# First FFT stage of the later batches with the data stationary, turned by DMA transposes instead of through DRAM

## The chip, the cores and the metric

The kernel runs on one core of a Trainium2 chip. The metric is the device time of one execution in microseconds. Three executions of the kernel before took 783.91, 784.35 and 784.50 us, median 784.35.

The engines that the text names: PE (TensorE, matrix multiplications; "PEld" are its weight loads), DVE (VectorE), ACT (ScalarE), POOL (GpSimd), and SP (SyncE), which only issues DMA transfers here. A matmul has a stationary operand, which is loaded into the array beforehand, and a moving operand, which streams through it; the result lands in PSUM, and DVE or ACT must carry it ("evacuate" it) into SBUF, the working memory.

## The reference

Eight sequences of 3008 tokens with 256 channels are filtered in the frequency domain along the sequence; the result goes through a two-layer network with a gated activation.

```
X = rfft(x, axis=1)                       # x: 8 x 3008 x 256
y = irfft(X * (filt_r + 1j*filt_i), n=3008, axis=1)
h = y.reshape(24064, 256) @ w_in          # 256 -> 2048
g = h / (1 + exp(-beta * h))
out = g @ w_out                           # 2048 -> 256, float32
```

## The kernel before

**The network** is the bulk. The 24064 tokens are cut into 47 blocks of 512, the 2048 hidden units into 16 slices of 128. One step is one slice of one block: two matmuls of 512 columns into hps (L842), a SILU on ACT into gT (L857), and, two steps later (LAG), four matmuls of 256 columns that add gT times a slice of w_out onto acc (L897). After 16 steps acc is evacuated into ost and stored. The matmul order on PE is the order in which the Python loop emits it; nothing is reordered by a scheduler.

**The filtering** of one batch feeds the blocks of that batch and is woven into the steps of the batch before it. The transform of 3008 points is factored as 94 rows of 32 (S = 47 x 64, J = 32 columns j):

1. s1 (L623): for each j, the 94 rows are multiplied with the 94x96 table t1, which gives 96 = 4 x 24 rows (four parts a for 24 frequencies k).
2. s23 (L644): for each frequency k, the 128 = 32 x 4 rows (j, a) are multiplied with a 128x128 table (L651), then with the filter (p_t, q_t on DVE, v_t on POOL), then with the table of the inverse (L677).
3. s4 (L692): the last stage back to the sequence (last4, L553, matmul L556).

Between 1 and 2 the data must change its partition axis: s1 leaves the 96 rows (a, k) on the partitions, s23 wants (j, a) there. The kernel before does this through DRAM. Two columns j at a time go through one matmul with the table stationary and 512 columns moving (L629); the evacuation puts them into an a1 tile of eight columns j, and SP writes it to the DRAM scratch d1 (L634). Once all four are written, a2_read (L636) reads d1 back in four groups of six frequencies with (j, a) on the partitions (L641). Between 2 and 3 there is a like round trip through d2 (L682, L689), which stays as it is.

Batch 0 is different: it works alone at the start, and its first stage (first1, L298) already holds the data stationary (L305) and turns it with PE transposes (turn_a, L396). It isn't changed.

**The order.** A plan written by hand says in which step each piece goes (place, L706; the calls from L764 on). For batch 1: s1 in steps 3 to 14, then in the next step a2_read(1) and, right behind it on SP, the last eight of the twelve loads of the real filter (uf, L741; each 256 KB, frequencies in groups of eight); s23 starts in step 20. For batch 2: s1 in steps 52 to 66, a2_read in step 75. For the later ones, with a the first step of the batch before: s1 from a + 48, a2_read at a + 68, and s23 from 3 steps after the next batch's own start, a span of about 30 steps. SP's queue runs in order: d1 and d2 transfers, filter loads and the stores of ost share it.

**Buffers that the steps touch.** apool has three a1 tiles, a2pool five a2 tiles (four for a batch), ostp three ost tiles (a block fills two), fpsum three PSUM banks for all filter stages, opsum three for acc.

**The end.** The last block has four accumulators of 256 columns (h = 0 to 3); ACT evacuates 0 and 3, DVE 1 and 2; the third store is issued from ACT's queue, the others from SP.

Of the kernel before, what the change touches and what calls it, by code (L numbers as in the profile page):

```python
# [9 lines left out]
P = 128  # L10
# [3 lines left out]
F32 = mybir.dt.float32  # L14
BF16 = mybir.dt.bfloat16
# [13 lines left out]
NK = 24  # L29
J = 32  # L30
KG = 6
NG = NK // KG
JG = 8
# [6 lines left out]
def kernel(  # L40
# [10 lines left out]
    nc = tc.nc  # L51

    B, S, D = x.shape
# [5 lines left out]
    NDC = D // P  # L59
    NFB = FF // P  # L60
    NP = 2 * N1
    KP = 4 * NK
# [6 lines left out]
    dpool = ctx.enter_context(tc.tile_pool(name="dram_scratch", bufs=2, space=bass.MemoryType.DRAM))  # L69

    def pool(name, bufs, **kw):
        return ctx.enter_context(tc.tile_pool(name=name, bufs=bufs, **kw))
# [1 line left out]
    consts = pool("consts", 1)  # L74
    wpool = pool("wpool", 1)
    xpool = pool("xpool", 1)
    apool = pool("apool", 3)
    ypool = pool("ypool", 2)
    a2pool = pool("a2pool", 5)
    pqpool = pool("pqpool", 3)  # L80
# [5 lines left out]
    fpsum = pool("fpsum", 3, space=bass.MemoryType.PSUM)  # L86
# [4 lines left out]
    t1 = consts.tile([NP, KP], BF16, name="t1", tag="t1")  # L91
    t4 = consts.tile([KP, NP], BF16, name="t4", tag="t4")
    t1b = consts.tile([NP, KP], BF16, name="t1b", tag="t1b")
# [13 lines left out]
    def evac(dst, src, on_act, scale=None):  # L107
        if on_act:
            nc.scalar.activation(dst, src, ACT.Copy, scale=1.0 if scale is None else scale)  # L109
        elif scale is None:  # L110
            nc.vector.tensor_copy(dst, src)  # L111
        else:
            nc.vector.tensor_scalar_mul(dst, src, scale)  # L113
# [132 lines left out]
    half = fixed("half", -0.5)  # L246
# [289 lines left out]
    ys = {}  # L536
    ys[0] = ypool.tile([P, NDC, NK * P], BF16, name="y", tag="y")
    zz0 = {}
    zz0[0] = apool.tile([KP, JG, D], BF16, name="zz", tag="a1")


    def turn_z(g, i, on_act=False):
# [67 lines left out]
    st = {}  # L610

    def start(b):
        d1 = dpool.tile([J, KP, D], BF16, name="d1", tag="d1")
        d2 = dpool.tile([J, KP, D], BF16, name="d2", tag="d2")
        st[b] = {
            "x": xs.pop(b),
            "d1r": d1.rearrange("j r d -> r j d"),
            "d2r": d2.rearrange("j r d -> r j d"),
            "d1c": d1.rearrange("j (a k) d -> (j a) k d", a=4),
            "d2c": d2.rearrange("j (a k) d -> (j a) k d", a=4),  # L620
        }

    def s1(b, i, on_act):  # L623
        s = st[b]
        g, jj = divmod(2 * i, JG)
        if jj == 0:
            s["a1"] = apool.tile([KP, JG, D], BF16, name="a1", tag="a1")
        ps = fpsum.tile([P, 512], F32, name="ps1", tag="f")
        nc.tensor.matmul(  # L629
            ps[:KP], lhsT=t1[:], rhs=s["x"][:, 2 * i : 2 * i + 2, :], start=True, stop=True  # L630
        )
        evac(s["a1"][:, jj : jj + 2, :], ps[:KP], on_act)
        if jj + 2 == JG:
            nc.sync.dma_start(s["d1r"][:, g * JG : (g + 1) * JG, :], s["a1"][:])  # L634

    def a2_read(b):  # L636
        s = st[b]
        s["a2"] = []
        for h in range(NG):
            t = a2pool.tile([P, KG, D], BF16, name="a2", tag="a2")  # L640
            nc.sync.dma_start(t[:], s["d1c"][:, h * KG : (h + 1) * KG, :])  # L641
            s["a2"].append(t)

    def s23(b, i):  # L644
        s = st[b]
        if i < NK // 2:
            k0 = 2 * i
            g, kk = divmod(k0, KG)
            ps = fpsum.tile([P, 2, D], F32, name="ps2", tag="f")
            for e in range(2):  # L650
                nc.tensor.matmul(  # L651
                    ps[:, e, :],
                    lhsT=t2[:, k0 + e, 3:5, :].rearrange("p c k -> p (c k)"),
                    rhs=s["a2"][g][:, kk + e, :],
                    start=True,
                    stop=True,
                )
            p_t = pqpool.tile([P, 2, D], F32, name="p_t", tag="p_t")
            q_t = pqpool.tile([P, 2, D], F32, name="q_t", tag="q_t")
            v_t = vpool.tile([P, 2, D], BF16, name="v_t", tag="v_t")  # L660
            ks_ = slice(k0, k0 + 2)
            nc.vector.tensor_tensor(p_t[:], ps[:], frr[:, ks_, :], ALU.mult)  # L662
            nc.vector.scalar_tensor_tensor(  # L663
                q_t[M:P], ps[:M], -1.0, fri[M:P, ks_, :], ALU.mult, ALU.mult
            )
            nc.vector.tensor_tensor(q_t[:M], ps[M:P], fri[M:P, ks_, :], ALU.mult)  # L666
            nc.gpsimd.tensor_tensor(v_t[:], p_t[:], q_t[:], ALU.add)  # L667
            s["v", i] = v_t
        if i >= VLAG:
            k0 = 2 * (i - VLAG)  # L670
            g, kk = divmod(k0, KG)
            if kk == 0:
                s["z"] = zpool.tile([P, KG, D], BF16, name="z", tag="z")
            v_t = s.pop(("v", i - VLAG))
            ps = fpsum.tile([P, 2, D], F32, name="ps3", tag="f")
            for e in range(2):
                nc.tensor.matmul(  # L677
                    ps[:, e, :], lhsT=t3[:, k0 + e, :], rhs=v_t[:, e, :], start=True, stop=True
                )
            evac(s["z"][:, kk : kk + 2, :], ps[:], True)  # L680
            if kk + 2 == KG:
                nc.sync.dma_start(s["d2c"][:, g * KG : (g + 1) * KG, :], s["z"][:])  # L682
# [114 lines left out]
            place(a + 68, a + 68, [lambda b=b: a2_read(b + 1)], per=9)  # L797
        place(a + 63, a + 78, u4(b))

    def store(t0, tn, ost, eng=nc.sync):  # L800
        if t0 >= S:
            eng.dma_start(
                out[t0 : t0 + tn, :].rearrange("(c p) d -> p c d", p=P), ost[:, : tn // P, :]
            )
            return
        for tb in range(tn // P):
            c0 = t0 + tb * P
            c1 = c0 + P
            while c0 < c1:
                lo = (c0 - t0) % P  # L810
                if c0 >= S:
                    nc.sync.dma_start(out[c0:c1, :], ost[lo : lo + c1 - c0, tb, :])
                    break
                g, r = divmod(c0, CLS)
                n = min(c1 - c0, CLS - r)
                nc.sync.dma_start(
                    AP(
                        out.tensor,
                        out.offset + (r // JC * J + g * JC) * D,
                        [[J * D, n // JC], [D, JC], [1, D]],  # L820
                    ),
                    ost[lo : lo + n, tb, :],
                )
                c0 += n
# [4 lines left out]
    for s in range(len(steps) + LAG):  # L829
# [34 lines left out]
        if s >= LAG:  # L864
# [40 lines left out]
            if fb == NFB - 1:  # L905
                for h, a in enumerate(acc):
                    if h * per % 2 == 0:
                        ost = ostp.tile([P, 2, D], F32, name="ost", tag="ost")
                    c = h * per % 2
                    on_act = h == 0 and i < 6 or last and h in (0, 3)  # L910
                    evac(ost[:, c : c + per, :], a[:], on_act)
                    eng = nc.scalar if last and h == 2 else nc.sync
                    store(t0 + h * per * P, per * P, ost[:, c : c + per, :], eng)


# [28 lines left out]
```

## Time and profile before

| | us |
|---|---|
| median of 3 executions | 784.35 |
| the profiled execution | 783.44 |
| its span, first to last instruction | 781.4 |
| PE busy | 772.4 |
| ACT busy | 595.8 |
| DVE busy | 390.8 |
| L857 SILU on ACT | 515.6 |
| L897 and L842 matmuls | 451.4 and 447.7 |
| L629 matmuls, 112 of them | 42.0 |
| a1 evacuations on DVE, 96 of them | 65.9 |

Busy matmul time is the union of intervals that overlap, since each matmul is counted until its result has drained; what a matmul takes from PE is the distance to the start of the next. The granted TensorE clock was full in the whole run. Transfers issued by SP show their issue in the trace, not their landing; a landing is seen only where an engine waits for it.

### The profile page before, as it was taken

The page shows a single profiled execution, that of the slowest core. Times are in us where ns is not written, and L with a number is a line of the kernel's source. Part 1 is how long each engine was busy: PE and PEld are TensorE (multiplying, and loading weights), DVE is VectorE, ACT ScalarE, POOL GpSimd, SP SyncE. Part 2 cuts the span into 40 slices and gives each one's busy share as a digit, 9 for nine tenths or more (in the row PEclk, how much of TensorE's full clock was granted, in tenths as well). Part 3 has the DMA queues.
Part 4 walks back from the last instruction along what each step waited for, and adds up shares of the span by engine and source line. Part 5 has one row for each costly group of instructions (what it writes and reads, how often), then busy time and mean ns, then how long its engine had stood idle before and what let it go on. Part 6 is the DMA issues. An engine that isn't in the chain of part 4 may idle for free.

```text
span 781.4 us, 15550 instructions
## 1 busy us (share of the span) xinstructions
PE 772.4 (99%) x6108; PEld 548.5 (70%) x6108; DVE 390.8 (50%) x640; ACT 595.8 (76%) x926; POOL 142.9 (18%) x145
## 2 busy tenths in 40 slices
PE   8999999999999999999999999999999999999997
PEld 5866667766777667876678766787667776776665
DVE  7847646746446553474635746277453751401001
ACT  7887887886678867787677876778767787677776
POOL 7523401420013100231002310034000330000000
PEclk9999999999999999999999999999999999999999
DMA  8968673517801286022951238412471114100101
GB/s 190 261 168 226 161 219 123 132 63 202 222 28 68 79 206 188 29 91 92 198 159 37 86 124 181 140 56 88 118 199 55 48 68 128 55 29 28 55 28 54
DMA packets 84473, 91.45 MB, mean 117 GB/s; under 512 B 4562, under 2 KB 74596, under 8 KB 83442
## 3 DMA queue, kind: packets, MB, share of 16 engines
q1 hardware_dynamic: 81536, 74.61, 31.0%
q0 software_dynamic: 2720, 15.73, 10.4%
q8 instruction: 47, 0.77, 0.4%
q14 instruction: 26, 0.21, 0.1%
q10 hardware_dynamic: 144, 0.13, 0.0%
HBM read 57.16 MB, written 46.66 MB: 133 GB/s over the span
## 4 chain that ended last, share of the span: by engine, by line
PE 95%; ACT 2%; DVE 1%; DMA 1%; issue 0%; DVEq 0%; ACTq 0%; POOL 0%; POOLq 0%; SPq 0%
PE acc L897 41%; PE hps L842 41%; PE ps L629 3%; PE ps L556 3%; PE ps L677 2%; PE ps L651 2%; PE psz L477 1%; ACT a L109 0%; DMA a<-d 0%; DMA d<-a 0%; ACT gT L857 0%; PE pb L403 0%; ACT a_t L109 0%; ACT t L280 0%; ACT r L284 0%
## 5 line engine op out<-in xcount | busy, mean ns | idle before, releaser
L857 ACT ACTIVATE gT<-hps,beta_sb 128x512 bf16<-128x512 f32 x752 | 515.6, 687 | 172.4 <-PE hps L842 160.7
L897 PE MATMUL acc<-wout_sb,gT 128*128 128x256 bf16 x3008 | 451.4, 272 | 0.0
L842 PE MATMUL hps<-y,win_sb 128*128 128x512 bf16 (+8 forms) x1730 | 447.7, 351 | 0.0
L897 PEld LDWEIGHTS <-gT 128*128 128x128 bf16 x3008 | 285.6, 98 | 128.8 <-issue 0.3
L842 PEld LDWEIGHTS <-win_sb 128*128 128x128 bf16 x1730 | 164.9, 98 | 24.4 <-issue 0.2
L667 POOL TENSOR_TENSOR v_t<-p_t,q_t 128x512 bf16<-128x512 f32 x84 | 106.6, 1269 | 389.8 <-DVE q_t L666 382.7
L111 DVE COPY ost<-acc 128x512 f32<-128x512 f32 (+1 forms) x88 | 56.2, 677 | 191.4 <-PE acc L897 188.2
L111 DVE CAST a<-ps 96x512 bf16<-96x512 f32 x96 | 65.9, 687 | 85.2 <-PE ps L629 84.6
L113 DVE TENSOR_SCALAR y<-ps 128x376 bf16<-128x376 f32 (+1 forms) x115 | 61.6, 543 | 58.8 <-PE ps L556 58.8
L662 DVE TENSOR_TENSOR p_t<-ps,frr 128x512 f32<-128x512 f32 x84 | 58.1, 691 | 36.9 <-PE ps L651 31.6
L666 DVE TENSOR_TENSOR q_t<-ps,fri 64x512 f32<-64x512 f32 x84 | 58.3, 694 | 1.2
L663 DVE SCALAR_TENSOR_TENSOR q_t<-ps,fri 64x512 f32<-64x512 f32 x84 | 57.5, 684 | 1.1
L556 PEld LDWEIGHTS <-zz 96*128 96x128 bf16 x512 | 35.3, 97 | 29.1 <-issue 0.3
L109 ACT ACTIVATE z<-ps 128x512 bf16<-128x512 f32 x84 | 49.5, 589 | 0.0
L629 PE MATMUL ps<-xg,t 94*96 94x512 bf16 x112 | 42.0, 381 | 0.1
L556 PE MATMUL ps<-t,zz 96*128 96x94 bf16 x448 | 36.7, 204 | 0.0
L677 PE MATMUL ps<-v_t,t 128*128 128x256 bf16 x168 | 32.1, 273 | 0.4 <-ACT y L109 0.4
L651 PE MATMUL ps<-a,t 128*128 128x256 bf16 x168 | 32.1, 273 | 0.3 <-DMA a<-d 0.3
L120 POOL DMA_DIRECT2D xg<-in_x_dram x22 | 12.1, 552 | 100.9 <-PE acc L897 96.8
L651 PEld LDWEIGHTS <-t 128*128 128x128 bf16 x168 | 15.6, 98 | 14.7 <-DMA a<-d 0.8
L629 PEld LDWEIGHTS <-t 94*96 94x96 bf16 x112 | 13.7, 123 | 12.0
L677 PEld LDWEIGHTS <-t 128*128 128x128 bf16 x168 | 16.2, 98 | 6.9 <-ACT y L109 0.7
(118 smaller groups left out, 194.9 us busy)
## 6 DMA issues: line engine op xcount, KB each, us to landing
out_dram<-ost SPq DMA_DIRECT2D x80, 256.0 KB
d<-a SPq DMA_DIRECT2D x28, 384.0 KB
a<-d SPq DMA_DIRECT2D x28, 384.0 KB
d<-z SPq DMA_DIRECT2D x28, 384.0 KB
zz<-d SPq DMA_DIRECT2D x28, 384.0 KB
xg<-in_x_dram POOLq DMA_DIRECT2D x6, 1280.0 KB, 10.4
frr<-in_filt_r_dram SPq DMA_DIRECT2D x12, 256.0 KB
out_dram<-ost SPq DMA_DIRECT2D x19, 128.0 KB
```

The source lines that it names most:

```text
L111: nc.vector.tensor_copy(dst, src)
L113: nc.vector.tensor_scalar_mul(dst, src, scale)
L556: nc.tensor.matmul(ps[:, e, :NP], lhsT=zz[:, jj + e, dc * P : (dc + 1) * P], rhs=tab[:], start=True, stop=True,)
L629: nc.tensor.matmul(ps[:KP], lhsT=t1[:], rhs=s["x"][:, 2 * i : 2 * i + 2, :], start=True, stop=True)
L651: nc.tensor.matmul(ps[:, e, :], lhsT=t2[:, k0 + e, 3:5, :].rearrange("p c k -> p (c k)"), rhs=s["a2"][g][:, kk + e, :], start=True, stop=True,
L662: nc.vector.tensor_tensor(p_t[:], ps[:], frr[:, ks_, :], ALU.mult)
L666: nc.vector.tensor_tensor(q_t[:M], ps[M:P], fri[M:P, ks_, :], ALU.mult)
L667: nc.gpsimd.tensor_tensor(v_t[:], p_t[:], q_t[:], ALU.add)
L677: nc.tensor.matmul(ps[:, e, :], lhsT=t3[:, k0 + e, :], rhs=v_t[:, e, :], start=True, stop=True)
L842: nc.tensor.matmul(hps[:, pos - t0 : pos - t0 + ln], lhsT=win_sb[:, dc, fb * P : (fb + 1) * P], rhs=ys[b][:, dc, n0 : n0 + ln], start=(dc ...
L857: nc.scalar.activation(gT[:, :tn], hps[:, :tn], ACT.Silu, scale=beta_sb[:, fb : fb + 1])
L897: nc.tensor.matmul(acc[tb // per][:, tb % per, :], lhsT=g_[:, tb * P : (tb + 1) * P], rhs=wout_sb[:, f_, :], start=(f_ == 0 and tb % per = ...
```

## The change

First stage, batches 1 to 7: for each group of four columns j and each half of the channels (dc), four matmuls hold 128 channels of x stationary (94x128) and move the 94x96 table t1b, whose columns are ordered (k, a). The result has the channels on the partitions. One evacuation of 128x384 puts it into an a1 tile of its half, ordered (k, j, a). For batch 1 the two halves alternate; for later batches the first half is done whole, then the second. In a2_read eight DMA transposes, issued by SP, turn each half's six blocks of 128x128 per frequency group into a2, where (j, a) is on the partitions; L651 reads the two halves of a2 as one operand of 256 columns. d1 is gone. apool has two tiles, each now holding half the channels of a whole batch.

At the end, accumulator 3 is evacuated in two halves, one on DVE and one on ACT, and the third store goes out from SP like the others.

```diff
-    apool = pool("apool", 3)
+    apool = pool("apool", 2)
...
     def start(b):
-        d1 = dpool.tile([J, KP, D], BF16, name="d1", tag="d1")
...
-            "d1r": d1.rearrange("j r d -> r j d"),
+            "a1": [apool.tile([P, NK * P], BF16, name="a1", tag="a1") for _ in range(NDC)],
...
     def s1(b, i, on_act):
         s = st[b]
-        g, jj = divmod(2 * i, JG)
-        if jj == 0:
-            s["a1"] = apool.tile([KP, JG, D], BF16, name="a1", tag="a1")
-        ps = fpsum.tile([P, 512], F32, name="ps1", tag="f")
-        nc.tensor.matmul(
-            ps[:KP], lhsT=t1[:], rhs=s["x"][:, 2 * i : 2 * i + 2, :], start=True, stop=True
+        jq, dc = divmod(i, NDC) if b == 1 else divmod(i, J // 4)[::-1]
+        ps = fpsum.tile([P, 4, P], F32, name="ps1", tag="f")
+        for e in range(4):
+            nc.tensor.matmul(
+                ps[:, e, :KP],
+                lhsT=s["x"][:, 4 * jq + e, dc * P : (dc + 1) * P],
+                rhs=t1b[:],
+                start=True,
+                stop=True,
+            )
+        dst = s["a1"][dc].rearrange("p (k j a) -> p j k a", j=J, a=4)
+        evac(
+            dst[:, 4 * jq : 4 * jq + 4],
+            ps[:, :, :KP].rearrange("p j (k a) -> p j k a", a=4),
+            on_act,
         )
-        evac(s["a1"][:, jj : jj + 2, :], ps[:KP], on_act)
-        if jj + 2 == JG:
-            nc.sync.dma_start(s["d1r"][:, g * JG : (g + 1) * JG, :], s["a1"][:])
 
     def a2_read(b):
         s = st[b]
         s["a2"] = []
-        for h in range(NG):
-            t = a2pool.tile([P, KG, D], BF16, name="a2", tag="a2")
-            nc.sync.dma_start(t[:], s["d1c"][:, h * KG : (h + 1) * KG, :])
+        for g in range(NG):
+            t = a2pool.tile([P, NDC, KG, P], BF16, name="a2", tag="a2")
+            for dc in range(NDC):
+                nc.sync.dma_start_transpose(
+                    t[:, dc],
+                    s["a1"][dc][:, g * KG * P : (g + 1) * KG * P],
+                )
             s["a2"].append(t)
...
-                    rhs=s["a2"][g][:, kk + e, :],
+                    rhs=s["a2"][g][:, :, kk + e, :],
...
-                    on_act = h == 0 and i < 6 or last and h in (0, 3)
-                    evac(ost[:, c : c + per, :], a[:], on_act)
-                    eng = nc.scalar if last and h == 2 else nc.sync
-                    store(t0 + h * per * P, per * P, ost[:, c : c + per, :], eng)
+                    on_act = h == 0 and i < 6 or last and h == 0
+                    if last and h == nch - 1:
+                        for half in range(2):
+                            cols = slice(half * P, (half + 1) * P)
+                            evac(ost[:, c : c + per, cols], a[:, :, cols], half == 1)
+                    else:
+                        evac(ost[:, c : c + per, :], a[:], on_act)
+                    store(t0 + h * per * P, per * P, ost[:, c : c + per, :])
```

More of the change, by code (lines that the diff above doesn't have):

```diff
@@ L538 @@
     zz0 = {}
-    zz0[0] = apool.tile([KP, JG, D], BF16, name="zz", tag="a1")
+    zz0[0] = apool.tile([P, NK * P], BF16, name="zz", tag="a1")
+    zz0[0] = zz0[0][:KP, : JG * D].rearrange("p (j d) -> p j d", j=JG)
     def turn_z(g, i, on_act=False):
@@ L616, in start @@
             "x": xs.pop(b),
-            "d1r": d1.rearrange("j r d -> r j d"),
+            "a1": [apool.tile([P, NK * P], BF16, name="a1", tag="a1") for _ in range(NDC)],
             "d2r": d2.rearrange("j r d -> r j d"),
-            "d1c": d1.rearrange("j (a k) d -> (j a) k d", a=4),
             "d2c": d2.rearrange("j (a k) d -> (j a) k d", a=4),
@@ L798, with store @@
         place(a + 63, a + 78, u4(b))
-    def store(t0, tn, ost, eng=nc.sync):
+    def store(t0, tn, ost):
         if t0 >= S:
-            eng.dma_start(
+            nc.sync.dma_start(
                 out[t0 : t0 + tn, :].rearrange("(c p) d -> p c d", p=P), ost[:, : tn // P, :]
```

## The prediction

> **What bounds it now.** I read the page first: busy times, then the chain that ended last, the groups and the DMA queues.
>
> ```profile
> PE 772.4 (99%) x6108; PEld 548.5 (70%) x6108; DVE 390.8 (50%) x640; ACT 595.8 (76%) x926; POOL 142.9 (18%) x145
> ...
> q1 hardware_dynamic: 81536, 74.61, 31.0%
> ...
> PE 95%; ACT 2%; DVE 1%; DMA 1%; issue 0%; DVEq 0%; ACTq 0%; POOL 0%; POOLq 0%; SPq 0%
> PE acc L897 41%; PE hps L842 41%; PE ps L629 3%; PE ps L556 3%; PE ps L677 2%; PE ps L651 2%; PE psz L477 1%; ACT a L109 0%; DMA a<-d 0%; DMA d<-a 0%; ACT gT L857 0%; PE pb L403 0%; ACT a_t L109 0%; ACT t L280 0%; ACT r L284 0%
> ...
> L629 PE MATMUL ps<-xg,t 94*96 94x512 bf16 x112 | 42.0, 381 | 0.1
> L556 PE MATMUL ps<-t,zz 96*128 96x94 bf16 x448 | 36.7, 204 | 0.0
> ```
>
> PE is the bound: 95% of the chain, idle almost nowhere. So a microsecond of matmul removed is a microsecond gained, and anything else matters only when it makes PE wait. L629 is the stage that is rewritten. Its 381 ns is a latency, not the time it takes from PE; for that I take distances between starts in the timeline of PE. First L629 in the steady stretch:
>
> ```profile
> 106.65 0.59 PE L842 MATMUL hps<-y,win_sb 128*128 128x512 bf16 x2
> 107.08 0.38 PE L629 MATMUL ps<-xg,t 94*96 94x512 bf16 x1
> 107.30 0.60 PE L897 MATMUL acc<-wout_sb,gT 128*128 128x256 bf16 x4
> ```
>
> One L629 takes 107.30 - 107.08 = 0.22 us (216 ns: the eight 512-wide warm-up matmuls from 7.62 give (1.89 - 0.38)/7). The new form already runs in batch 0 (first1, L305: same operands and sizes):
>
> ```profile
> 6.51 0.51 PE L305 MATMUL psa<-t1b,xg 94*128 94x96 bf16 x8
> 6.85 0.60 PE L189 MATMUL pw<-wz 128*128 128x512 bf16 x2
> ```
>
> Eight take 6.85 - 6.51 = 0.34 us, 42 ns each with their weight loads; sixteen from 12.03 give (0.84 - 0.206)/15 = 42.3 ns. The stage-4 matmuls (L556) do the same between the big ones: four start at 63.26 and the next group starts at 63.42, 0.16 us.
>
> Then the SyncE queue and the one wait on this data:
>
> ```profile
> 57.77 1.77 SPq L641 DMA_DIRECT2D a<-d  x4
> 59.71 0.34 SPq L133 DMA_DIRECT2D frr<-in_filt_r_dram  x1
> ...
> 61.29 0.11 PEld L651 LDWEIGHTS <-t 128*128 128x128 bf16 x2 [0.81 <-DMA a<-d]
> 61.29 0.39 PE L651 MATMUL ps<-a,t 128*128 128x256 bf16 x2 [0.32 <-DMA a<-d]
> ```
>
> ```profile
> 204.98 1.85 SPq L641 DMA_DIRECT2D a<-d  x4
> 209.63 29.86 SPq L802 DMA_DIRECT2D out_dram<-ost  x6
> ```
>
> In batch 1 the round trip (write 3.06 us, read 3.47 us in the chain) ends 0.3 us late for PE. In batch 3 it is issued at 204.98 and first used (L651) at 223.86: 19 us of cover. Behind it on SyncE stand the filter loads (59.71, batch 1) and the output stores (209.63). Windows of 2 us show how full the DMA engines are: batch 1 has no room, later batches have plenty.
>
> ```profile
> 70.00:72.00 2.00, 2.00 (x17) 1.44 (x15) 1.62 (x3) 2.00 (x4) 0.73 (x1) 1.00 1.02 218
> ...
> 214.00:216.00 2.00, 2.00 (x16) 1.34 (x14) 0.00 (x0) 1.64 (x3) 0.00 (x0) 1.00 0.00 0
> ```
>
> **What the Trainium skill says.** "TensorE: Matmul & The Clock Gate", Back-to-back issue gap, gives N/2.4 + 2.5 ns per matmul: 216 ns for 512 columns and 42.5 ns for 96, as the trace has it. The same section puts a stream of weight-load and matmul pairs at about 81 ns for 128 columns; the trace disagrees at 96 columns (42 ns). No row of the kernel before is a DMA transpose. "DMA: Bandwidth & Descriptors", Latency and other measured facts, gives an effective 261 GB/s for one; "VectorE: DVE Perf Modes", The three transpose paths, gives 1309 ns for one 128x128 block.
>
> **The change part by part.**
>
> *Matmuls.* 112 L629 of 216 ns go (16 for each of 7 batches); 112 groups of four at 4 x 42.4 = 170 ns come: -112 x 0.046 = **-5.2 us**, all on the chain. The weight load of each hides under the matmul before it, as in L305 and L556; if that cover failed, see rival D.
>
> *Evacuations.* 96 DVE casts of 687 ns (96x512) become 128x384 with a scattered output, which batch 0 shows at 544 ns on DVE and 482 on ACT (before: 586). DVE gets 96 x 0.14 = 14 us back, ACT 16 x 0.1. Neither sets the end: 0.
>
> *Round trip.* Per batch four writes and four reads of 384 KB go; eight transposes of 192 KB, one after the other on SyncE, come. Call one transpose T (per instruction, issue and move, whichever is slower). Below: 196,608 bytes at 261 GB/s is 0.75 us. Nearest row: q1 took 0.31 x 16 x 781.4 us for 81,536 packets, 47.5 ns each (mean 915 bytes); 768 pieces of 256 bytes over 16 engines at that price are 2.3 us. Above: six blocks at 1.309 us, 7.9 us. The packets are smaller than that mean, so I take **T = 1.65 us**, about midway between the first two, 13.2 us per batch; the upper end stays in the range.
>
> *Batch 1.* The last evacuation ends at 54.6 now, 0.7 earlier after (16 x 0.046): transposes from 53.9. The first pair lands near 53.9 + 3.3 + 1 for completion = 58.2 (estimate), before PE asks at about 60.3: the 0.3 us wait goes, **-0.3 us**. Late next are the last eight filter loads, which stand behind all eight transposes. Now they begin at 59.7 and keep the engines full until 74, so the first four (filter rows 8 to 15) take about 6.5 us. After, these land at 53.9 + 8T + 6.5; DVE needs them at 73.4 (product 4). Behind that product on DVE are its own two others and the evacuation after; its PSUM bank is one of three of fpsum, and PE wants it back at 75.9 for product 5, 0.5 us after DVE frees it now. The stall is thus about 8T - 13: 0.2 us at T = 1.65, 3 us at 2, 5.4 at 2.3. I add **+0.2 us**.
>
> *Batches 2 to 7.* The first pair needs 2T < 19 us, the next pairs less (product 3 at 232.6: 4T < 27). The stores at 209.6 now go out behind the transposes: 205 + 8T + 2. Of the three ost buffers the second evacuation at 223.4 needs the first store's back: T < 2.05. Above that DVE waits, with the products queued behind; PE follows once those banks run out, about 6 us later, near T = 2.75, at about (8T - 22) us in each of six batches. At 1.65: 0. The two-deep a1 pool costs nothing: the next batch writes it some 70 us after these transposes.
>
> *Tail.* The last evacuation (ACT 0.38 us, 128x256) is split over DVE and ACT. From 683 and 418 ns for 512 and 256 columns DVE needs about 285 ns for 128, ACT about 280: **-0.1 us**. The third store moves from ACT's queue to SyncE's, free by then: 0.
>
> Sum: -5.2 - 0.3 + 0.2 - 0.1 = -5.4. Span 781.4 becomes 776.0; with the 2.04 us around it (783.44 - 781.4) 778.0 against that execution's 783.44. The median 784.35 lies 0.9 above it: **779.0 us**.
>
> **Rivals.**
>
> A, the forecast, T up to 1.65: 779. For it: the cover of 19 us, empty DMA engines after 212.
>
> B, batch 1 alone pays: T from 1.65 to 2.5, the filter loads late, stall 0.2 to 7 us: 779 to 786, no gain left at T = 2.3. For it: the packet price and the full engines; against it: packets of a quarter of that size.
>
> C, the transposes become the SyncE queue's bound: T over 2.5. They hold back stores, ost, then DVE, then PE. T = 3 gives 784.35 - 5.6 + 11 + 6 x 2 = 802; T = 4 gives 19 + 60, near 858. It decides from T = 2.3 by batch 1 and steepens from 2.75. For it: 1309 ns for one block of which each instruction has six; against it: 261 GB/s.
>
> D, between the big matmuls the quadruples run at 81 ns: 112 x (0.324 - 0.216) = +12 us, 796. L556 at 41 ns in that place speaks against it.
>
> **Numbers.** A 0.42, B 0.24, C 0.29, D 0.05. About 0.2% (1.6 us) is what a measurement of this kernel tells from no change. Of B 0.15 lies under T = 2.1 and is faster, 0.09 is within the bound; C and D are slower. Faster 0.57, same 0.09, slower 0.34. The range: below, 778 (the filter loads cost nothing and ACT's relief in batch 1 gives a little); above, 802, which leaves the worse part of C, 0.18, out. If A or B hold, 778 to 786.
>
> **What would show it.** The new matmul line: 448 in groups of four, 0.17 us from start to next start (D: 0.32). DMA transposes on SyncE: their spacing is T. In batch 1, no wait of L651 on the transposed tile; p_t at product 4 waiting, and fpsum users on PE behind it, would be B. The ost evacuations waiting on stores in batches 2 to 7, with PE idle, would be C. Without gaps on PE and without a gain, the matmul sum is wrong.

## The result

Faster by 0.9%, a little more than forecast. In six executions each the kernel before took 784.27 us (783.79 to 784.50) and the changed one 777.22 us (775.81 to 778.27): ratio 0.9909, 95% interval 0.9896 to 0.9921. The forecast was 779.0 with a range of 778 to 802, so the gain is 7.05 us instead of 5.4, and the time lies 0.8 us below the range. In the profiled executions 783.44 us became 777.06, and the span of 781.4 became 775.3. The ratios below leave out executions that ran slow, of which the first run below had three (795.76 to 1645.36 us) and the others none.

The page of the changed kernel: busy times, the main DMA queue, the chain by engine and by line, and the two groups of the new stage. In the changed kernel L852 is hps, L907 is acc, L628 the new first stage, L661 and L687 the two matmuls of the filter stage, L672 to L677 the products, L648 the transposes, and L812 and L826 stores.

```profile
PE 767.5 (99%) x6444; PEld 554.2 (71%) x6444; DVE 379.3 (49%) x641; ACT 594.9 (77%) x926; POOL 142.8 (18%) x145
...
q1 hardware_dynamic: 100496, 63.73, 30.8%
...
PE 97%; ACT 1%; DMA 1%; POOL 0%; DVE 0%; issue 0%; POOLq 0%
PE acc L907 42%; PE hps L852 42%; PE ps L557 3%; PE ps L628 2%; PE ps L687 2%; PE ps L661 2%; DMA xg<-in_x_dram 1%; PE psz L477 1%; PE pz L549 0%; ACT a L109 0%; ACT a_t L109 0%; PE pb L403 0%; POOL xg L120 0%; PE ps L451 0%; PE ps2q L451 0%; PE pt L354 0%
...
L111 DVE CAST a<-ps 128x384 bf16<-128x384 f32 x96 | 53.5, 558 | 91.4 <-PE ps L628 91.2
...
L628 PE MATMUL ps<-t1b,xg 94*128 94x96 bf16 x448 | 36.7, 205 | 0.0
```

PE still makes the chain, now 97% of it, and "DMA a<-d" and "DMA d<-a" have left the line list. The queue carries 10.9 MB less (63.73 for 74.61) in more packets, and its share of the engines is unchanged. The new matmul groups take what was forecast. The timeline of PE in the changed kernel shows four of them in 96.56 - 96.39 = 0.17 us:

```profile
96.39 0.33 PE L628 MATMUL ps<-t1b,xg 94*128 94x96 bf16 x4
96.56 0.60 PE L907 MATMUL acc<-wout_sb,gT 128*128 128x256 bf16 x4
```

The price that the forecast lacked, T, is the duration in the source view of L648 (min/median/max in ns, then first and last start):

```profile
L648 SPq DMA_TRANSPOSE a<-a x56: 1210/1287/6692, 53.0 to 578.6; - x56
```

A transpose holds SyncE for 1.29 us in the median (1.89 in the mean), where a plain read of a2 before held it for 0.38 in the median. Eight take 12 us in batch 1, with the filter loads behind them (SyncE's timeline, changed kernel):

```profile
52.97 12.04 SPq L648 DMA_TRANSPOSE a<-a  x8
65.18 0.44 SPq L133 DMA_DIRECT2D frr<-in_filt_r_dram  x1
```

In batch 3 they start at 191.86, where the reads of before were issued only at 204.98. The first two take 6.7 and 4.1 us there, beside a load of x that POOL issues at 189.90. Batches 4 to 6, which have such a load 2 us ahead too, look alike (17.9 to 19.5 us for the eight in batches 3 to 6); in batches 1, 2 and 7, which have none there, no transpose takes over 2.5. Yet in batch 3 all eight are issued before the first L661 of the batch at 221.5:

```profile
191.86 19.54 SPq L648 DMA_TRANSPOSE a<-a  x8
211.50 26.51 SPq L812 DMA_DIRECT2D out_dram<-ost  x6
```

**Where the time came from.** I set each remaining PE matmul of one trace beside the same one of the other, and noted each place where the distance between the two traces changes.

| place | us |
|---|---|
| 112 first-stage groups, 0.046 each | -5.20 |
| 41.6: PE no longer waits for an evacuation of the first stage | -0.25 |
| 61.3: the round trip is no longer late | -0.48 |
| 76.7: a filter group no longer waits for a PSUM bank | -0.55 |
| rest | +0.05 |
| first hps matmul to last matmul: 741.03 to 734.61 | -6.42 |
| start-up up to the first hps: 35.92 to 37.00 | +1.08 |
| last matmul to the end of the span: 4.45 to 3.67 | -0.78 |
| around the span: 2.04 to 1.76 | -0.28 |

The three waits are all in batch 1's stretch. In the timeline of PE, kernel before, two L629 take 0.69 us from their start to the next group instead of 0.43 (the second starts at 42.10, and in the built program it has the PSUM bank from which ACT carries an older group until 42.04), and L677 waits for ACT:

```profile
41.62 0.85 PE L629 MATMUL ps<-xg,t 94*96 94x512 bf16 x2
42.31 0.60 PE L897 MATMUL acc<-wout_sb,gT 128*128 128x256 bf16 x4
...
76.65 0.39 PE L677 MATMUL ps<-v_t,t 128*128 128x256 bf16 x2 [0.37 <-ACT y L109]
```

In the changed kernel the same places show no wait: eight L628 take 0.34 us, L661 starts straight after hps, and L687 straight after L661.

```profile
41.36 0.51 PE L628 MATMUL ps<-t1b,xg 94*128 94x96 bf16 x8
41.70 0.60 PE L907 MATMUL acc<-wout_sb,gT 128*128 128x256 bf16 x4
...
60.55 0.59 PE L852 MATMUL hps<-y,win_sb 128*128 128x512 bf16 x2
60.98 0.38 PE L661 MATMUL ps<-a,t 128*128 128x256 bf16 x2
...
75.58 0.38 PE L661 MATMUL ps<-a,t 128*128 128x256 bf16 x2
75.80 0.38 PE L687 MATMUL ps<-v_t,t 128*128 128x256 bf16 x2
```

### The profile page after: what moved, and what is told of

Its sections match the earlier page's. It is cut to its first block, busy times and chain, and to the rows that moved or that the text cites. A ratio compares the mean times of both kernels' runs of the same rounds, so it can differ in the third digit from the quotient of the medians.

```text
span 775.3 us, 16219 instructions
## 1 busy us (share of the span) xinstructions
PE 767.5 (99%) x6444; PEld 554.2 (71%) x6444; DVE 379.3 (49%) x641; ACT 594.9 (77%) x926; POOL 142.8 (18%) x145
## 3 DMA queue, kind: packets, MB, share of 16 engines
q1 hardware_dynamic: 100496, 63.73, 30.8%
## 4 chain that ended last, share of the span: by engine, by line
PE 97%; ACT 1%; DMA 1%; POOL 0%; DVE 0%; issue 0%; POOLq 0%
PE acc L907 42%; PE hps L852 42%; PE ps L557 3%; PE ps L628 2%; PE ps L687 2%; PE ps L661 2%; DMA xg<-in_x_dram 1%; PE psz L477 1%; PE pz L549 0%; ACT a L109 0%; ACT a_t L109 0%; PE pb L403 0%; POOL xg L120 0%; PE ps L451 0%; PE ps2q L451 0%; PE pt L354 0%
## 5 line engine op out<-in xcount | busy, mean ns | idle before, releaser
L907 PE MATMUL acc<-wout_sb,gT 128*128 128x256 bf16 x3008 | 451.6, 272 | 0.0
L852 PE MATMUL hps<-y,win_sb 128*128 128x512 bf16 (+8 forms) x1730 | 447.7, 351 | 0.0
L907 PEld LDWEIGHTS <-gT 128*128 128x128 bf16 x3008 | 279.6, 98 | 106.3 <-ACT gT L867 0.2
L852 PEld LDWEIGHTS <-win_sb 128*128 128x128 bf16 x1730 | 165.0, 98 | 24.4 <-issue 0.2
L677 POOL TENSOR_TENSOR v_t<-p_t,q_t 128x512 bf16<-128x512 f32 x84 | 106.7, 1270 | 383.9 <-DVE q_t L676 375.4
L111 DVE COPY ost<-acc 128x512 f32<-128x512 f32 (+2 forms) x89 | 56.6, 674 | 194.0 <-PE acc L907 188.4
L111 DVE CAST a<-ps 128x384 bf16<-128x384 f32 x96 | 53.5, 558 | 91.4 <-PE ps L628 91.2
L672 DVE TENSOR_TENSOR p_t<-ps,frr 128x512 f32<-128x512 f32 x84 | 58.1, 692 | 33.5 <-PE ps L661 30.9
L628 PEld LDWEIGHTS <-xg 94*128 94x128 bf16 x448 | 30.7, 97 | 23.4 <-issue 0.4
L628 PE MATMUL ps<-t1b,xg 94*128 94x96 bf16 x448 | 36.7, 205 | 0.0
L687 PE MATMUL ps<-v_t,t 128*128 128x256 bf16 x168 | 32.1, 273 | 0.0
L661 PE MATMUL ps<-a,t 128*128 128x256 bf16 x168 | 32.1, 273 | 0.0
L661 PEld LDWEIGHTS <-t 128*128 128x128 bf16 x168 | 15.7, 98 | 14.1
L687 PEld LDWEIGHTS <-t 128*128 128x128 bf16 x168 | 16.3, 98 | 6.4 <-DVE q_t L676 0.4
```

Source lines behind the costliest of these rows:

```text
L628: nc.tensor.matmul(ps[:, e, :KP], lhsT=s["x"][:, 4 * jq + e, dc * P : (dc + 1) * P], rhs=t1b[:], start=True, stop=True,)
L661: nc.tensor.matmul(ps[:, e, :], lhsT=t2[:, k0 + e, 3:5, :].rearrange("p c k -> p (c k)"), rhs=s["a2"][g][:, :, kk + e, :], start=True, sto ...
L687: nc.tensor.matmul(ps[:, e, :], lhsT=t3[:, k0 + e, :], rhs=v_t[:, e, :], start=True, stop=True)
L852: nc.tensor.matmul(hps[:, pos - t0 : pos - t0 + ln], lhsT=win_sb[:, dc, fb * P : (fb + 1) * P], rhs=ys[b][:, dc, n0 : n0 + ln], start=(dc ...
L907: nc.tensor.matmul(acc[tb // per][:, tb % per, :], lhsT=g_[:, tb * P : (tb + 1) * P], rhs=wout_sb[:, f_, :], start=(f_ == 0 and tb % per = ...
```

## Experiments

The theory: later batches gain only through matmul columns (0.046 us for each of 112 groups); batch 1 gains besides by three waits; the new end gives little. The rivals: the gain comes from the DRAM traffic that is gone, or from the end. "First hps to last matmul" below is the stretch of the table above; it leaves out start-up and end, which vary. Every run was timed beside the kernel before on the same chip.

### The new end alone

In the kernel before, only the end is the new one.

```diff
-                    on_act = h == 0 and i < 6 or last and h in (0, 3)
-                    evac(ost[:, c : c + per, :], a[:], on_act)
-                    eng = nc.scalar if last and h == 2 else nc.sync
-                    store(t0 + h * per * P, per * P, ost[:, c : c + per, :], eng)
+                    on_act = h == 0 and i < 6 or last and h == 0
+                    if last and h == nch - 1:
+                        for half in range(2):
+                            cols = slice(half * P, (half + 1) * P)
+                            evac(ost[:, c : c + per, cols], a[:, :, cols], half == 1)
+                    else:
+                        evac(ost[:, c : c + per, :], a[:], on_act)
+                    store(t0 + h * per * P, per * P, ost[:, c : c + per, :])
```

> The kernel before with only the new end (accumulator 3 in two halves, third store from SP). The aligned traces give the new end 0.77 us: 0.25 because ACT no longer issues a store ahead of its last evacuation, -0.24 because the two halves run one after the other, 0.74 because the last store no longer meets an instruction fetch on a DMA engine. If the fetch belongs to the old end: 0.8 us less than before. If it was chance in that one execution: within 0.1 us of before, as the prediction had it.

783.52 us (783.36 without the three slow executions) beside 783.78, ratio 0.9994 [0.9985, 1.0002]; last matmul to end 4.21 us. No gain that the times can tell. The traces say why the halved evacuation gives nothing. The timeline of ACT at the end of the kernel before: ACT issues a store for 0.37 us and begins the last evacuation 0.29 us after the last matmul, which ends at 776.95.

```profile
776.68 0.37 ACTq L802 DMA_DIRECT2D out_dram<-ost  x1
777.24 0.38 ACT L109 ACTIVATE ost<-acc 128x256 f32<-128x256 f32 x1 [1.07 <-PE acc L897]
```

At the end of the changed kernel the last matmul ends at 771.61. These are the lines of DVE's half and then of ACT's half, from the timelines of the two engines:

```profile
771.65 0.29 DVE L111 COPY ost<-acc 128x128 f32<-128x128 f32 x1 [0.34 <-PE acc L907]
...
771.98 0.28 ACT L109 ACTIVATE ost<-acc 128x128 f32<-128x128 f32 x1 [1.14 <-DVE ost L111]
```

The halves run one after the other: 0.65 us from the last matmul to the end of the second, against 0.67 before.

### The third store on SyncE alone

```diff
-                    eng = nc.scalar if last and h == 2 else nc.sync
-                    store(t0 + h * per * P, per * P, ost[:, c : c + per, :], eng)
+                    store(t0 + h * per * P, per * P, ost[:, c : c + per, :])
```

> The kernel before with only the third store of the last block moved from ACT's queue to SP. Own theory: ACT's last evacuation starts 0.25 us earlier, behind the last matmul at once, so 0.25 us less, and up to 0.7 more if the fetch no longer meets the last store. The prediction's step: no difference.

784.0 us beside 783.78, ratio 1.0001 [0.9993, 1.0009]. The last evacuation does start earlier, 0.04 us after the last matmul (at 776.87) instead of 0.29:

```profile
776.91 0.38 ACT L109 ACTIVATE ost<-acc 128x256 f32<-128x256 f32 x1 [0.82 <-PE acc L897]
```

Last matmul to end is 4.23 us. A quarter of a microsecond on the path of the last store is real in the trace and too small for the times.

### The changed kernel with the old end

The edit of the first run the other way round: the four lines of the old end stand in the changed kernel.

> The changed kernel with the end of the kernel before. Own theory: 6.4 to 7.1 us less than before, 0 to 0.8 more than the changed kernel. If the surplus over the forecast were all in the end, 5.3 us less than before.

776.25 us beside 783.78, ratio 0.9901 [0.9889, 0.9914], as good as the whole change; first hps to last matmul 734.53, last matmul to end 3.71. So the -0.78 of the table is not the work of the new end. What does differ is an instruction fetch: the DMA records of the kernel before hold an 8 KB fetch packet from 778.67 to 779.35, in the middle of the last stores, whose last packets land at 779.70, 2.75 us after the last matmul. In the changed kernel, with either end, no fetch falls there and they land 2.0 to 2.1 us after it. The view of DMA of the kernel before in the window 777 to 780, by queue:

```profile
q1 hardware_dynamic: 432, 0.39, 37.6%
q10 hardware_dynamic: 144, 0.13, 12.6%
q14 instruction: 1, 0.01, 1.4%
```

In the two runs before this one the fetch fell after the stores, at 780.7 to 781.3, but ahead of the end: their stores landed 2.1 us after the last matmul, and the closing part behind the stores took 2.1 us instead of 1.6 to 1.7. Over all thirteen traces of this study, eight have no fetch between the last matmul and the end, and these take 3.6 to 3.8 us for that stretch. The other five take 4.0 to 4.5, each with a fetch in it: four of 8 KB, and in the first trace of the bank experiment below (4.32) one of 16 KB, from 0.08 us before the last matmul's end to 0.88 after it. So the longer ends go with a fetch; that it is the cause is not shown, and what places it there wasn't tried.

### The new matmuls made as costly as the old ones

The new stage throughout, but the moving table is widened from 96 to 128 columns (32 are copies, which nothing reads), so that four matmuls have 512 columns like one L629. DRAM traffic, transposes and evacuations stay as in the changed kernel.

```diff
+    t1w = consts.tile([NP, P], BF16, name="t1w", tag="t1w")
+    gp.tensor_copy(t1w[:, :KP], t1b[:])
+    gp.tensor_copy(t1w[:, KP:], t1b[:, : P - KP])
...
-                ps[:, e, :KP],
+                ps[:, e, :],
...
-                rhs=t1b[:],
+                rhs=t1w[:],
```

> The changed kernel, each of the four matmuls of the first stage moving 128 columns instead of 96 (the 32 more are not used), so that a group moves 512 columns as L629 did. DMA transposes, evacuations and the new end stay. If the gain of the later batches is matmul time: a group takes 4 x 55.5 = 222 ns (batch 0's 128-column transposes: (0.83 - 0.22)/11), 112 x 0.052 = 5.8 us more than the changed kernel, 1.2 us less than before. If it is the DRAM traffic that went away: 5 to 7 us less than before.

782.50 us beside 784.12, ratio 0.9986 [0.9976, 0.9997]; first hps to last matmul 740.55, 5.94 more than in the changed kernel and 0.48 less than before. The timeline of PE, this kernel:

```profile
96.52 0.39 PE L631 MATMUL ps<-t1w,xg 94*128 94x128 bf16 x4
96.74 0.60 PE L910 MATMUL acc<-wout_sb,gT 128*128 128x256 bf16 x4
```

Four take 0.22 us now, so that 112 x 0.052 = 5.8 us come back. With the columns back, nearly the whole gain of the stretch is gone, though d1 stays gone: the traffic that was saved is worth nothing by itself in batches 2 to 7. The medians keep more, 1.6 us; in the profiled executions most of the rest is the end, 3.67 us for 4.45 before.

### Batch 1 alone, and the others alone

Both have the old end. In the first, batch 1 uses the new stage and batches 2 to 7 go through DRAM; the second is its mirror image (the a1 pool is shared, and has two buffers).

```diff
+    def start(b):
+        (new_start if b == 1 else old_start)(b)
+
+    def s1(b, i, on_act):
+        (new_s1 if b == 1 else old_s1)(b, i, on_act)
+
+    def a2_read(b):
+        (new_a2_read if b == 1 else old_a2_read)(b)
...
-                    rhs=s["a2"][g][:, :, kk + e, :],
+                    rhs=s["a2"][g][:, :, kk + e, :] if s["new"] else s["a2"][g][:, kk + e, :],
```

> The new first stage and the DMA transposes for batch 1 alone, the DRAM round trip for batches 2 to 7, and the old end. Own theory from the aligned traces: 16 x 0.046 = 0.74 of matmul, 0.48 of the round trip's late landing, 0.25 of one PSUM wait in the first stage, 0.55 of the bank of the inverse matmul: 2.0 us less than before. By the prediction's sum for batch 1: 0.74 + 0.3 = 1.0 us less.

781.69 us beside 784.12, ratio 0.9966 [0.9955, 0.9978]; first hps to last matmul 739.01, 2.02 less than before. That is 16 x 0.046 = 0.74 for the columns and 0.25 + 0.48 + 0.55 = 1.28 for the waits.

> The complement: batch 1 through DRAM as before (two buffers for its first tiles in place of three), batches 2 to 7 new, old end. Own theory: 96 x 0.046 = 4.5 us less than before and the three waits of batch 1 stay. Matmul alone explains the later batches if so; if the round trips of later batches cost PE anything, more than 4.5.

778.37 us beside 784.12, ratio 0.9925 [0.9914, 0.9937]; first hps to last matmul 736.96, 4.07 less than before. 96 x 0.046 are 4.42; the round trip of batch 1 comes 0.6 us later than before, which would leave 3.8 (the other 0.26 I can't place, and whether the third a1 buffer that is missing delays that round trip wasn't tried), and the wait for the bank is still there (timeline of PE, L702 and L728 are the two matmuls of the filter stage):

```profile
62.01 0.39 PE L702 MATMUL ps<-a,t 128*128 128x256 bf16 x2 [0.94 <-DMA a<-d]
...
77.36 0.39 PE L728 MATMUL ps<-v_t,t 128*128 128x256 bf16 x2 [0.37 <-ACT y L109]
```

The two parts add up to 6.09 of the 6.42 us, and a third of it belongs to one of seven batches.

### The wait for a bank, without the new stage

In the built programs, L677 at 76.65 writes into the PSUM bank from which ACT is still carrying y, the output of the matmul group just before: fpsum gave both bank 5 (a trace doesn't show banks). To move the choice without the new stage, the kernel before has four evacuations of batch 0 on DVE instead of ACT:

```diff
-    units = uz(3, True)
+    units = uz(3, False)
```

> The kernel before with the last four evacuations of batch 0's last stage on DVE instead of ACT. The build then gives the inverse matmul of batch 1 (third in the group behind product 5) a PSUM bank other than the one its neighbour has just filled. Own theory: the 0.55 us that PE lost there was that bank, so the wait of L677 on the y evacuation goes and 0.5 us with it. Rival: the wait came from ACT being busy there and moves to another instruction, no difference.

783.12 us beside 783.78, ratio 0.9991 [0.9981, 1.0]. A second measurement:

> The same edit of the kernel before as in the earlier run (the last four evacuations of batch 0's last stage on DVE, which gives the following product group another PSUM bank), for a second reading. Theory (a bank chosen at build time costs 0.55 us at 76.65): 0.5 us faster than before, 783.5 beside 784.1, and in the trace the second matmul group of the filter in batch 1 waits for nothing. Rival (the 0.55 us belongs to the old first stage): no change.

782.58 us beside 784.11, ratio 0.9981 [0.9972, 0.9991]. In both traces 0.53 us come back at this place, and the group waits for nothing (second trace, timeline of PE):

```profile
76.76 0.38 PE L651 MATMUL ps<-a,t 128*128 128x256 bf16 x2
76.98 0.38 PE L677 MATMUL ps<-v_t,t 128*128 128x256 bf16 x2
```

The edit also takes from ACT the very evacuation that PE waited for. But on DVE it ends later, at 77.91 in the second trace, when the group at 76.98 has long started; so an earlier evacuation is not why the wait is gone.

Neither profiled execution as a whole gained from it. In the second the round trip came 0.7 us later than in the trace of before, and a load of x cost it 0.5. The first took 787.38 us, the longest of its fourteen executions: ACT waited 3.1 us for a write of d2, PE then 2.5 us for a SILU, and after that the clock was at half from 95.5 to 98.9, some 4 us in all (timeline of PE, and one window of 2 us, in which the granted clock stands after the five busy columns).

```profile
91.29 0.60 PE L897 MATMUL acc<-wout_sb,gT 128*128 128x256 bf16 x4
94.42 0.59 PE L842 MATMUL hps<-y,win_sb 128*128 128x512 bf16 x2 [2.54 <-ACT gT L857]
...
96.00:98.00 2.00, 2.00 (x10) 1.09 (x8) 1.87 (x3) 1.19 (x3) 0.00 (x0) 0.50 0.24 69
```

The edit explains none of this. The bank explains the wait in every kernel that I looked at: where the two groups have the same bank (before, 5 and 5; batch 1 by DRAM, 5 and 5; the next experiment, 6 and 6) the wait is there, where they differ (the changed kernel, 6 and 5; batch 1 alone, 6 and 5; the wide table and this one, 5 and 7) it isn't. So this half microsecond is a by-product of which bank the pool gives in the program as it is built, not of the transposes.

### Every transpose twice

The changed kernel, with each transpose issued a second time into a spare tile that nothing reads (it takes the fifth of the a2 buffers). This nearly doubles SyncE's time: 22.7 us in batch 1, 23.0 in batch 2, 29.5 to 30.1 in batches 3 to 6 and 23.7 in batch 7.

```diff
+        dump = a2pool.tile([P, NDC, KG, P], BF16, name="dump", tag="a2")
...
-                nc.sync.dma_start_transpose(
-                    t[:, dc],
-                    s["a1"][dc][:, g * KG * P : (g + 1) * KG * P],
-                )
+                for to in (dump[:, dc], t[:, dc]):
+                    nc.sync.dma_start_transpose(
+                        to,
+                        s["a1"][dc][:, g * KG * P : (g + 1) * KG * P],
+                    )
```

> The changed kernel with every DMA transpose issued twice, the extra one into a spare tile. One took SP 1.29 us, so T is doubled to about 2.7. The prediction's formula for batch 1, 8T - 13, gives a stall of 8 us there by the late filter loads: 8 us more than the changed kernel, 1 us more than before, with DVE's p_t of product 4 waiting. Batches 2 to 7 by the prediction at T = 2.7: next to nothing; by rival C about 10 us more each once T exceeds 2.75.

795.84 us beside 784.12, ratio 1.0153 [1.0138, 1.0168]; first hps to last matmul 19.2 us more than in the changed kernel. The loss sits in the stretches of batches 1 and 2 alone: counted from the first hps, 12.9 us by 110 in the changed kernel's time, 19.0 by 150, and 19.2 at the last matmul.

Batch 1, from the timelines of SyncE, PE and DVE in this order of time: the last transpose and the first filter load, the last matmul of PE before its pause, the product that waits for the filter, and the matmul that ends the pause.

```profile
73.18 2.34 SPq L650 DMA_TRANSPOSE a<-a  x1
75.63 0.51 SPq L133 DMA_DIRECT2D frr<-in_filt_r_dram  x1
...
79.92 0.38 PE L663 MATMUL ps<-a,t 128*128 128x256 bf16 x2
...
83.66 0.69 DVE L674 TENSOR_TENSOR p_t<-ps,frr 128x512 f32<-128x512 f32 x1 [10.99 <-DMA frr<-in_filt_r_dram]
...
85.81 0.61 PE L689 MATMUL ps<-v_t,t 128*128 128x256 bf16 x2 [5.51 <-DVE q_t L678]
```

This is the mechanism of rival B. But DVE's product is 83.66 - 73.06 = 10.6 us later than in the changed kernel, and PE stops for only 5.5: it has about 5 us of other work before it needs that product. PE then pays a second time. These are windows of 2 us of this kernel; after the five busy columns come the granted clock, the DMA share and GB/s:

```profile
82.00:84.00 2.00, 0.00 (x0) 0.00 (x0) 0.34 (x1) 0.00 (x0) 0.00 (x0) 1.00 1.08 221
84.00:86.00 2.00, 0.19 (x2) 0.13 (x2) 1.73 (x3) 0.00 (x0) 0.08 (x1) 0.63 1.02 210
86.00:88.00 2.00, 2.00 (x9) 1.14 (x8) 0.00 (x0) 0.60 (x1) 1.19 (x1) 0.50 1.09 299
88.00:90.00 2.00, 2.00 (x9) 1.13 (x8) 1.34 (x2) 0.76 (x2) 0.00 (x0) 0.50 0.47 155
...
92.00:94.00 2.00, 1.98 (x18) 1.26 (x16) 1.94 (x4) 1.84 (x4) 1.98 (x4) 1.00 0.36 141
```

After the pause the clock is at half for some 5.5 us of PE's work (to 91.35), nine matmuls in 2 us instead of eighteen, which costs another 2.7 (the distance to the changed kernel's trace grows by that much from 79.3 to 81.9). The Trainium skill ("TensorE: Matmul & The Clock Gate", What's actually happening) says that the clock is halved after an idle window of about 3.4 us, and full again after about as long of sustained work. After the pause of 5.5 us the trace agrees in kind, though half clock lasted longer. As a limit for a single pause the 3.4 us don't hold here: half clock also followed the pause of 2.5 us in the first trace of the experiment above, while the pause of 2.6 us at 106 in this one brought none. A late load of x, that pause at 106, adds 2.7 more, and the rest of the 12.9 are pauses of 0.5 to 0.7 ahead of it: the first transposed pair late at 61, a load of x, and the bank of the experiment above, which this program chose alike for both groups again.

In batch 2 the sixteen transposes hold the stores (126.1 to 149.1 on SyncE), and rival C appears: DVE's timeline has a 9 us wait of an ost evacuation for a store, and PE's the pause that follows.

```profile
159.80 0.69 DVE L111 COPY ost<-acc 128x512 f32<-128x512 f32 x1 [9.00 <-DMA out_dram<-ost]
...
162.67 0.38 PE L663 MATMUL ps<-a,t 128*128 128x256 bf16 x2 [4.28 <-DVE q_t L678]
```

Of the 6.1 us that batch 2 loses, 4.4 are this pause and 1.7 the half clock behind it (163.0 to 166.4).

In batches 3 to 7 nothing is lost even at double cost, though in 3 to 5 DVE waits 3.1 to 4.5 us for a store too. There the transposes start 29.6 us before the first L663 of the batch, in the changed kernel as in this one, against 13.3 us in batch 2. The reads of before had 17.3 to 19.4 us in batches 3 to 6, and the prediction counted 19. That the earlier start is what spares PE is read from these distances; no run moves it.

### The two halves in two tiles

The changed kernel, with the two halves of the last accumulator in tiles and stores of their own, in case they were serial because they share ost.

```diff
-                            evac(ost[:, c : c + per, cols], a[:, :, cols], half == 1)
+                            part = gpool.tile([P, P], F32, name="part", tag="gT")
+                            evac(part[:], a[:, 0, cols], half == 1)
+                            r0 = t0 + h * P
+                            eng = nc.scalar if half else nc.sync
+                            eng.dma_start(out[r0 : r0 + P, cols], part[:])
```

> The changed kernel, but the two halves of the last accumulator go into two tiles of their own, and each half is stored by itself, one from SyncE and one from ACT, so that the halves need not wait for each other. In the changed kernel they ran one after the other: 0.61 us from the last matmul's end to the end of ACT's half. Theory (the halves are serial only because they share one tile): both start within 0.1 us of the last matmul and end about 0.3 us after it, so that the distance from the last matmul to the end falls by about 0.3 us, 776.9 us beside 777.2; too little for the times to tell, so the trace decides. Rival (the halves are serial for another reason, the accumulator's bank being read by two engines): ACT's half still starts only after DVE's.

776.95 us beside 784.11, ratio 0.9907 [0.9893, 0.992]. The rival held. From the timelines of DVE and ACT, with the last matmul ending at 770.46:

```profile
770.57 0.29 DVE L111 COPY part<-acc 128x128 f32<-128x128 f32 x1 [0.41 <-PE acc L907]
...
770.95 0.28 ACT L109 ACTIVATE part<-acc 128x128 f32<-128x128 f32 x1 [1.27 <-DVE part L111]
```

ACT waits for DVE still; what they still share is the accumulator. The Trainium skill ("PSUM — Partial Sum Buffer", PSUM bank collisions raise a hardware error) says that two engines must not touch one bank of the same partitions at once, reads included, and that schedulers order them; the order is what the trace shows, the error no run here.

### The changed kernel again

Unaltered.

> The changed kernel once more, unaltered, for a second measurement of the gain and a second trace of its start and its end. Theory (of the 7.05 us between the medians about 6.4 belong to the kernels, the rest to where the start-up and an instruction fetch near the end happen to fall): 6.0 to 7.5 us faster than before, and a first hps matmul and an end that differ from the first trace by some tenths. Rival (all 7 us belong to the kernels): the same start and end as in the first trace.

776.05 us beside 784.11, ratio 0.99 [0.9886, 0.9913]. In the trace the first hps is at 36.64 (37.00 in the first trace), the wait of 0.37 us for x at 47.4 is new, and last matmul to end is 3.67 as in the first. The start-up wanders: the first hps lies between 35.92 and 36.08 in the five traces whose programs have no new stage, and between 35.94 and 37.20 in the eight with it. The new ones tend to wait longer there for the first load of x (in the weight loads of L305, up to 3.4 us in all, against 1.1 at most), but one with 2.2 us of such waits started at 35.98. Whether a later start belongs to the change or to chance stays open; with the start counted out, the stretch took 735.05 us here, 0.44 more than in the first trace, for that wait for x.

## Why the prediction was right and wrong

**Matmuls, -5.2: right.** 0.046 us for each of 112 groups, -5.20 together. The widened table returned 5.94 us; rival D (81 ns a pair) is out, at 0.17 us for four.

**Evacuations, "Neither sets the end: 0": wrong by 0.25.** For batches 2 to 7 it holds. In batch 1 the groups come in pairs, with ACT evacuating too, and PE waited once at 41.6 for a bank: 0.69 us instead of 0.43 for the two L629, the second 0.05 us behind the end of ACT's evacuation. No separate run tests this; it is read from the two traces, and the sum for batch 1 alone (2.02) needs it.

**The round trip of batch 1, -0.3: right in kind, 0.48 in size.** I took the idle time that the line shows, 0.32. It is counted from the end of the matmul before, which lies after the end of its turn on PE: that one is the second of the pair at 60.37, starts at 60.59 and takes 0.22, so that the pause is 61.29 - 60.59 - 0.22 = 0.48.

```profile
60.37 0.59 PE L842 MATMUL hps<-y,win_sb 128*128 128x512 bf16 x2
```

The 1 us for completion in that term was a guess. In the run with doubled transposes the first pair was issued by 58.16 and PE waited for it until 61.5, about 3.3 us. With that, the pair of the changed kernel (issued by 55.99) would land at about 59.3, an estimate, and still ahead of L661 at 60.98.

**What was missing, 0.55 at 76.65.** The step that failed is the count of waits in batch 1, at the start of the prediction: I followed "the one wait on this data" and left out waits in the same stretch on other data. The wait of L677 for ACT stood in the timeline of before (0.37), as large as the one that I did count. That the change would remove it could not be read from the diff; the banks in the two built programs show it.

**The filter-load stall, "8T - 13", +0.2: wrong, 0.** T was 1.29 in the median instead of 1.65, and the eight of batch 1 took 12.0 us; the formula gives less than nothing there, and the product at 73.06 waited for its matmul and not for its filter (DVE's timeline, changed kernel).

```profile
73.06 0.69 DVE L672 TENSOR_TENSOR p_t<-ps,frr 128x512 f32<-128x512 f32 x1 [0.93 <-PE ps L661]
```

Its slope was tested by the double: with 22.8 us up to the first filter load (52.84 to 75.63) it gives 9.8 us for DVE, and 10.6 were measured. Its second half was wrong: PE wants the bank not 0.5 us after DVE frees it, but some 5 us, so the price for PE began later than I said, and then came with half a clock on top.

**Batches 2 to 7, 0: right, in part by luck.** In batches 3 to 6 the eight took 17.9 to 19.5 us, 2.2 to 2.4 each, above the T < 2.05 from which I said that DVE would wait. It didn't, since they started earlier than I had counted: those of batch 3 were through at 211.4. The thresholds, which I gave for all six batches alike from a cover of 19 us, are wrong. At the double rival C's (8T - 22) forecasts 1 to 2 us in batches 2 and 7 and about 8 in each of batches 3 to 6. Measured were 6 us in batch 2, through the stores as C says and with half a clock on top, and none in batches 3 to 7, which have 29.6 us of cover (191.86 to 221.49): the transposes need no round trip and start earlier.

**Tail, -0.1: the new end is worth nothing that can be told** (0.9994 [0.9985, 1.0002]). Halving the evacuation gives nothing because the halves run in turn, which I hadn't seen; the 0.25 us of ACT's issue, which I put at 0, is real but small. The profile's 0.78 comes with the changed kernel whichever end it has; the longer end of before goes with an instruction fetch.

For PE's stretch the sum was -5.3 (matmuls, round trip, filter loads) and -6.42 was measured: the missing 1.1 are 0.25 + 0.18 + 0.55 for the waits and 0.2 for the stall that didn't come, less 0.05 of rest. The medians say 7.05 here, and 7.2 to 8.1 in the three other comparisons of kernels with the whole new stage (old end, two tiles, again): in the profiled executions what goes beyond 6.42 lies at the end and around the span, and a late start takes a varying part of it back; for the others this is not shown. The range failed at its low end: it had almost no room for gains at waits. Its upper end, 802, is the sum at T = 3, though the text says that the 7.9 us of the dearest price stay in the range.

## What to carry to other kernels

Where one engine is the bound, list every wait of that engine in the stretch that an edit rebuilds, not only those on the data that is moved: here three waits of 0.25 to 0.55 us in one batch made a fifth of the gain, and one of them hung on the bank that a pool happened to give. A step's cover is counted from where its inputs are ready on the new path, not from where the old step was issued: here that was 10 to 12 us more in batches 3 to 6, where a doubled cost wasn't felt. And when one measures a saving at the very end of a program, the old end in the new kernel is the comparison that counts.

## What the hardware showed

A transpose of 128x768 in two bytes between tiles on chip held SyncE's queue for 1.29 us in the median, against 0.38 for a plain transfer of twice the size. The first two of a batch took up to 6.7 us beside a large load from POOL's queue, in each of the four batches that had one there and in none of the other three. What stands behind them in the queue waits that long.

A pause of PE of 5.5 us was followed by half clock, which cost 2.7 us more; one of 2.5 us in another trace was followed by 3.4 us of half clock, and one of 2.6 us by none.

Two evacuations from one accumulator, on DVE and ACT, ran one after the other, into one tile and into two.

An 8 KB instruction fetch took 0.68 us amid the last stores of the kernel before, and they landed 2.75 us after the last matmul instead of the 2.0 to 2.1 of most others.
